# First gate and up weights on a second DMA queue, later loads held, and all roots on GpSimd

## The chip, the cores and the metric

The kernel runs on one core of one Trainium2 chip. The metric is the device time of the whole program in microseconds (us), median of several executions. A profiled execution gives a span that is about 1.7 us shorter than its time, because it runs from the first to the last recorded instruction; times inside the kernel are counted from the start of that span.

TensorE multiplies matrices, VectorE and ScalarE do elementwise work, GpSimd some of the small work. Each takes its instructions in the order in which the program emitted them; below, a normalisation that is ready stands behind statistics that wait 1.49 us for their load. Loads are issued by SyncE, and after the change also by ScalarE; each issuer has a queue of its own (q1 and q10).

## The reference

```python
x = A_x                                   # (1, 2048, 512), bf16
xn = _layernorm(x, axis=-1)               # (x - mean) / sqrt(var + 1e-5)
return x + _A_ref(xn, A_w_r, A_w_i) + _B_ref(xn, B_w_gate, B_w_up, B_w_down)

# _A_ref: irfft2(rfft2(xn) * (w_r + 1j * w_i)), a spectral filter
# _B_ref: g = xn @ w_gate (512 x 1792); u = xn @ w_up (512 x 1792)
#         (gelu_tanh(g) * u) @ w_down (1792 x 512)
```

The rows of x come as 16 tiles of 128 rows, called x0 to x15 here. What matters is the head of the kernel: before TensorE can start on the gate and up products, x0 must be loaded, normalised, transposed on TensorE and copied out of PSUM, and the first 512 columns of `w_gate` (Wg) and `w_up` (Wu) must have landed. One such piece of weights is 512 KB, one tile of x is 128 KB.

## The kernel before

The program does not emit its work directly. It adds operations, with a modelled duration, a key and modelled landing times of the loads (`LAND`, `WG_LAND`, `WU_LAND`), to a list scheduler, which fixes one order per engine.

All first loads are on one queue, in this order:

```python
pin(nc.scalar.activation(out=root[:], in_=eps_t[:], func=AF.Sqrt, ...))  # loads the Sqrt table
load_x(0, 1)
load_x(1, 1)
nc.sync.dma_start(out=idx_t[:], in_=...)      # a table of row numbers, 12 bytes per row
load_w(Wg_sb, 0, 512)
load_w(Wu_sb, 0, 512)
load_x(2, 2)
load_w(Wg_sb, 512, 1024)
load_w(Wu_sb, 512, 1024)
load_x(4, 2)
# [...] more loads
LAND = {0: 2.9, 1: 3.5, 2: 8.8, 3: 8.8}
```

TensorE "spins" on zeros while it waits (N is the number of columns of a product's result). The aim is that its clock is released, that is, let up to full speed, before the real products come. In the traces the starts of products of N=128 are 0.107 us apart at half speed and 0.056 at full speed.

```python
for k in range(25):                           # 20 products of N=128, then 5 of N=512
    pin(nc.tensor.matmul(sp_ps[:, :P if k < 20 else D], lhsT=spin[:],
                         rhs=spin[:] if k < 20 else x_t[:, 0, :], start=True, stop=True))
```

The order on VectorE for the first two tiles (`after=o.get("last")` chains them):

```python
stats(0); mean(0)                             # mean also adds the Sqrt on ScalarE
stats(1)                                      # stands ahead of the first normalisation
recip(0); xn_(0, 0); mean(1); xn_(0, 1)       # xn in two halves of 256 columns
T(0, 0); T(0, 1)                              # transposes on TensorE
add("PE", 0.65, spin_on, ...)                 # six more spin products
copy(0, 0); copy(0, 1)                        # both on VectorE
# [...] the same for tile 1
```

Tiles 2 and 3 follow, with a root by Newton steps on VectorE; then come units of work. A unit is the gate product into a PSUM buffer of tag "G", the gelu of it on ScalarE, the up product into a buffer of tag "U", and on VectorE the product of the two, which frees "U":

```python
g = split("g_ps", "G", Wg_sb, ...)            # acquires one of 2 "G" buffers
u = split("u_ps", "U", Wu_sb, ...)            # acquires one of 2 "U" buffers
ge = add("ACT", ..., f_ge, [g], ..., acq=("ge",), rel=("G",))
h = add("DVE", ..., f_h, [ge, u], ..., rel=("U", "ge"), after=hold.get(k))
```

There are two "U" buffers, so the third up product waits until the first `h` has been done.

## Time and profile before

| | before |
|---|---|
| time, median of 3 (lowest to highest) | 179.57 us (179.57 to 179.84) |
| span of the profiled execution | 177.5 us |
| TensorE busy | 172.1 us, 97 % |
| first gate product starts | 6.34 us |
| first up product starts | 7.79 us |

Engine table of the kernel before: busy us, share of the span, number of instructions.

```profile
PE 172.1 (97%) x1115; PEld 96.0 (54%) x1133; DVE 116.6 (66%) x261; ACT 96.5 (54%) x171; POOL 20.1 (11%) x60
```

TensorE (PE) is the bound. It can only be helped where it idles or works on zeros, that is before about 7.8 us, and at one wait in the middle.

Timeline of VectorE (DVE) before: start us, duration us, engine, line, operation, output<-input, shapes, count, and in brackets the idle time before it with what ended it.

```profile
3.00 0.69 DVE L338 BATCH_NORM_STATS2 stats<-x_t 128x6 f32<-128x512 bf16 x1 [1.99 <-DMA x_t<-in_A_x_dram]
3.82 0.66 DVE L338 BATCH_NORM_STATS2 stats<-x_t 128x6 f32<-128x512 bf16 x1
...
4.58 0.35 DVE L344 TENSOR_SCALAR xn<-x_t,mv,rstd 128x256 bf16<-128x256 bf16 x1
...
8.44 1.29 DVE L338 BATCH_NORM_STATS2 stats<-x_t 128x6 f32<-128x512 bf16 x2 [1.69 <-DMA x_t<-in_A_x_dram]
...
11.46 0.69 DVE L515 TENSOR_TENSOR hT<-u_ps,ge 128x512 bf16<-128x512 f32 x1
```

x0's statistics start at 3.00, x1's at 3.82 with no wait, the first normalisation at 4.58. x2 and x3 land near 8.44, and the first `hT` product (the `h` above) comes at 11.46.

Timeline of TensorE before, same columns.

```profile
5.29 0.56 PE L350 MATMUL tp<-ident_t,xn 128*128 128x128 bf16 x4
...
6.34 0.61 PE L505 MATMUL g_ps<-xnT,Wg_sb 128*128 128x128 bf16 x8
...
7.79 1.07 PE L505 MATMUL u_ps<-xnT,Wu_sb 128*128 128x128 bf16 x16
8.69 1.06 PE L505 MATMUL g_ps<-xnT,Wg_sb 128*128 128x128 bf16 x16
9.59 1.06 PE L505 MATMUL u_ps<-xnT,Wu_sb 128*128 128x128 bf16 x16
10.48 1.91 PE L505 MATMUL g_ps<-xnT,Wg_sb 128*128 128x256 bf16 x16
12.23 0.60 PE L505 MATMUL u_ps<-xnT,Wu_sb 128*128 128x256 bf16 x4
```

Sixteen products of N=128 take 1.07 us, their starts 0.056 us apart: full speed. The 16 gate products of N=256 are two units of 8.

The waits of TensorE before (us in total, times, longest), and two pieces of its chain of waits (start us, us, what).

```profile
PE bp L581 <- ACT Bs L551: 0.4, 1, 0.4
```

```profile
2.65 5.09 DMA Wu_sb<-in_B_w_up_dram
...
7.79 1.07 PE u_ps L505 x16
```

The chain starts with the first up weights, issued at 2.65 and landed 5.09 us later. The wait of 0.4 us (0.45 in the timeline, at 40.4 us) is for a spectral evacuation on ScalarE.

### The profile page before, as it was taken

How to read it: one execution, taken by the hardware profiler on the slowest of the kernel's cores; microseconds unless marked ns; L12 is line 12 of the kernel's file. 1: busy time of each engine (PE TensorE's matmuls, PEld its weight loads, DVE VectorE, ACT ScalarE, POOL GpSimd, SP SyncE). 2: the span in 40 equal slices, each digit the busy share in tenths (PEclk: the TensorE clock that was granted, in tenths of full speed). 3: DMA queues.
4: the chain of work that ended last, by engine and by line, in shares of the span. 5: the costliest groups of instructions: out<-in, count | busy, mean ns of one | idle time of the engine just before them, and what ended most of it. 6: DMA issues, size and time to landing. Idle time of an engine off the chain costs nothing.

```text
span 177.5 us, 3118 instructions
## 1 busy us (share of the span) xinstructions
PE 172.1 (97%) x1115; PEld 96.0 (54%) x1133; DVE 116.6 (66%) x261; ACT 96.5 (54%) x171; POOL 20.1 (11%) x60
## 2 busy tenths in 40 slices
PE   7999999998999999999999999999999999999993
PEld 5798845464455554555555545454445444444463
DVE  3499999873933599998699999543526334344333
ACT  4463286979575989799999955453112111211200
POOL 1000534810676000000000000000000000000000
DMA  3999994243282752121202520200132222221212
GB/s 92 350 382 378 368 180 92 59 98 55 60 291 95 245 173 59 33 55 31 63 6 55 148 60 5 59 0 4 51 97 89 72 78 63 89 85 62 78 44 59
DMA packets 21872, 19.36 MB, mean 109 GB/s; under 512 B 8480, under 2 KB 20000, under 8 KB 21856
## 3 DMA queue, kind: packets, MB, share of 16 engines
q1 hardware_dynamic: 21440, 17.84, 34.6%
q0 software_dynamic: 416, 1.32, 2.5%
q8 instruction: 9, 0.15, 0.3%
q14 instruction: 7, 0.06, 0.1%
HBM read 13.38 MB, written 2.10 MB: 87 GB/s over the span
## 4 chain that ended last, share of the span: by engine, by line
PE 83%; ACT 5%; DMA 3%; issue 3%; POOL 2%; DVE 1%; SPq 1%; ACTq 0%
PE y_ps L820 27%; PE u_ps L505 23%; PE g_ps L505 22%; DMA Wu_sb<-in_B_w_up_dram 3%; PE dp L639 2%; ACT Bs L551 2%; PE yp L772 2%; PE gp L742 2%; PE y_ps L824 2%; PE ep L648 2%; ACT xn L467 2%; ACT ge L510 1%; DVE hT L515 1%; PE bp L581 1%; POOL t L366 0%
## 5 line engine op out<-in xcount | busy, mean ns | idle before, releaser
L505 PE MATMUL u_ps<-xnT,Wu_sb 128*128 128x512 bf16 (+2 forms) x267 | 56.9, 341 | 0.3
L505 PE MATMUL g_ps<-xnT,Wg_sb 128*128 128x512 bf16 (+2 forms) x265 | 56.4, 340 | 0.4
L515 DVE TENSOR_TENSOR hT<-u_ps,ge 128x512 bf16<-128x512 f32 x56 | 38.5, 688 | 19.0 <-PE u_ps L505 10.5
L820 PE MATMUL y_ps<-Wd_sb,hT 128*128 128x512 bf16 (+2 forms) x246 | 50.6, 355 | 0.3
L510 ACT ACTIVATE ge<-g_ps 128x512 bf16<-128x512 f32 x56 | 33.9, 606 | 21.4 <-PE g_ps L505 17.6
L505 PEld LDWEIGHTS <-Wu_sb 128*128 128x128 bf16 x272 | 24.9, 98 | 21.4 <-DMA Wu_sb<-in_B_w_up_dram 0.3
L505 PEld LDWEIGHTS <-Wg_sb 128*128 128x128 bf16 x272 | 24.8, 98 | 20.0
L820 PEld LDWEIGHTS <-hT 128*128 128x128 bf16 x252 | 23.2, 98 | 22.4
L778 ACT CAST yf<-yp 128x512 bf16<-128x512 f32 x16 | 9.3, 586 | 40.5 <-PE yp L772 40.5
L827 DVE TENSOR_TENSOR y_sb<-y_ps,y_sb 128x512 bf16<-128x512 f32 (+2 forms) x18 | 11.1, 631 | 30.0 <-PE y_ps L824 30.0
L653 ACT CAST E<-ep 64x512 bf16<-64x512 f32 x32 | 18.6, 580 | 1.3 <-PE ep L648 0.8
L338 DVE BATCH_NORM_STATS2 stats<-x_t 128x6 f32<-128x512 bf16 x16 | 10.5, 677 | 3.9 <-DMA x_t<-in_A_x_dram 3.9
L467 ACT ACTIVATE xn<-x_t,nb,rstd 128x512 bf16<-128x512 bf16 x12 | 9.7, 827 | 1.8 <-POOL nb L378 1.8
L551 ACT CAST Gs<-gp 128x512 bf16<-128x512 f32 x16 | 8.9, 592 | 0.9 <-PE gp L742 0.9
L551 ACT CAST ds<-dp 128x512 bf16<-128x512 f32 x16 | 9.0, 597 | 0.6 <-PE dp L639 0.5
L551 ACT CAST Bs<-bp 128x512 bf16<-128x512 f32 x16 | 8.4, 607 | 0.5 <-PE bp L581 0.5
L784 DVE TENSOR_TENSOR lv<-yf 128x512 bf16<-128x512 bf16 x16 | 6.1, 422 | 1.5 <-ACT yf L778 0.6
L772 PEld LDWEIGHTS <-Gs 128*128 128x128 bf16 x64 | 4.8, 98 | 3.5
L791 DVE TENSOR_TENSOR yt<-lv 128x512 bf16<-128x512 bf16 x16 | 6.1, 422 | 0.3
L824 PE MATMUL y_ps<-yt,RI_t 128*128 128x512 bf16 (+2 forms) x18 | 6.1, 355 | 0.0
L772 PE MATMUL yp<-CT,Gs 128*128 128x128 bf16 x64 | 6.0, 219 | 0.0
L742 PEld LDWEIGHTS <-F 128*128 128x128 bf16 x64 | 4.5, 98 | 2.6
(72 smaller groups left out, 123.2 us busy)
## 6 DMA issues: line engine op xcount, KB each, us to landing
F<-F SPq DMA_DIRECT2D x32, 64.0 KB, 2.0
y_sb<-in_A_x_dram SPq DMA_DIRECT2D x16, 128.0 KB, 2.1
out_dram<-y_sb SPq DMA_DIRECT2D x15, 128.0 KB, 1.7
x_t<-in_A_x_dram SPq DMA_DIRECT2D x7, 256.0 KB, 8.6
Wd_sb<-in_B_w_down_dram SPq DMA_DIRECT2D x1, 1792.0 KB, 7.5
Wg_sb<-in_B_w_gate_dram SPq DMA_DIRECT2D x2, 512.0 KB, 5.2
Wu_sb<-in_B_w_up_dram SPq DMA_DIRECT2D x2, 512.0 KB, 7.4
Wg_sb<-in_B_w_gate_dram SPq DMA_DIRECT2D x1, 768.0 KB, 10.4
```

Source lines behind the costliest of these rows:

```text
L338: V.bn_stats(out=st[:], in_=x_t[:, c, :])
L467: xn_op[c] = add("ACT", 0.72, lambda c=c: A.activation(out=xn[:, c, :], in_=x_t[:, c, :], func=AF.Identity, bias=nb[:, c:c + 1], scale=rst ...
L505: T_.matmul(b[name][:, f], lhsT=W_[:, e, (f0 + f) * P:(f0 + f + 1) * P], rhs=rhs[:, e, :], start=(e == 0), stop=(e == NE - 1))
L510: A.activation(out=b["ge"][:], in_=b["g_ps"][:], func=AF.Gelu_apprx_tanh)
L515: V.tensor_tensor(out=hT_of(sb, f0, m, o, w), in0=b["u_ps"][:], in1=b["ge"][:], op=ALU.mult)
L551: A.copy(out=o, in_=i)
L653: A.copy(out=b["E"][64 * h:64 * h + 64, r], in_=b["ep", h][64 * r:64 * r + 64])
L772: T_.matmul(t[:, q], lhsT=late["G"][:, q, c0 + j], rhs=IQ[q], start=(q == 0), stop=(q == 3), skip_group_check=True)
L778: A.copy(out=b["yf"][:, j], in_=b[j][:])
L820: T_.matmul(b[o][:], lhsT=hT_of(sb, f, 1, cl * P, P)[:, 0], rhs=Wd_sb[:, f, o:o + w], start=(f == 0), stop=False)
L824: T_.matmul(b[o][:], lhsT=late["RI"][:, c, :], rhs=late["yt"][:, c, o:o + w], start=False, stop=True)
L827: V.tensor_tensor(out=b["y"][:, o:o + w], in0=b[o][:], in1=b["y"][:, o:o + w], op=ALU.add)
```

## The change

Its intent: use the time before 7.8 us better. The first weights are to start at 0.8 us on ScalarE's queue instead of at 2.18 and 2.65 us; the later loads are held until the first root, so that they do not compete. The roots go to GpSimd's `pow`, so that ScalarE needs no Sqrt table and loads the gelu table early. The first unit is halved along its contraction, so that it can start on half of x0's transposed data.

```diff
-    pin(nc.scalar.activation(out=root[:], in_=eps_t[:], func=AF.Sqrt, bias=eps_t[:], scale=1.0))
+    nc.gpsimd.memset(Wg_sb[0:1, 0, 0:1], 0.0)            # before the identity is built
+    load_w(Wg_sb, 0, 512, nc.scalar)
+    load_w(Wu_sb, 0, 512, nc.scalar)
+    pin(nc.scalar.activation(out=warm[:], in_=eps_t[:], func=AF.Gelu_apprx_tanh))
     load_x(0, 1)
     load_x(1, 1)
-    nc.sync.dma_start(out=idx_t[:], ...)
-    load_w(Wg_sb, 0, 512)
-    load_w(Wu_sb, 0, 512)
-    load_x(2, 2)
-    load_w(Wg_sb, 512, 1024)
-    load_w(Wu_sb, 512, 1024)
+    def later_loads():
+        load_w(Wg_sb, 512, 1024)
+        load_x(2, 2)                                      # now behind the second gate weights
+        load_w(Wu_sb, 512, 1024)
+        # [...] the rest as before, idx_t late
-    LAND = {0: 2.9, 1: 3.5, 2: 8.8, 3: 8.8}
+    LAND = {0: 2.9, 1: 3.8, 2: 8.2, 3: 8.2}
-    for k in range(25):                                   # 20 x N=128, 5 x N=512
+    for k in range(32):                                   # 32 x N=128
# [...]
-            nc.tensor.matmul(sp_ps[:, :256], ...)         # spin_on
+            nc.tensor.matmul(sp_ps[:, :P], ...)
# [...] first_two():
         stats(0)
         mean(0)
         stats(1)
-        recip(0)
+        def rest():
+            nc.gpsimd.memset(Wg_sb[0:1, 0, 512:513], 0.0)
+        g = add("POOL", 0.15, rest, [o["root", 0]], key=-1999)
+        add("SP", 9.0, later_loads, [g], key=-1000)       # the hold
         xn_(0, 0)
-        mean(1)
         xn_(0, 1)
+        mean(1)
# [...]
+    def root(c0, n):                                      # for all tiles
+        nc.gpsimd.tensor_tensor(out=y, in0=y, in1=minus_half[:, 0:n], op=ALU.pow)
# [...] unit(): first unit halved, and the order of h on VectorE is free
+        if k == 0:
+            g = add("PE", occ / 2, lambda: mm_half(0), [xT_op[0, 0]], ...)
+            g = add("PE", occ / 2, lambda: mm_half(1), [xT_op[0], g], ...)
-        h = add("DVE", ..., rel=("U", "ge"), after=hold.get(k))
+        h = add("DVE", ..., rel=("U", "ge"))
```

Left out are the copies of the transposed halves (now one on VectorE, one on ScalarE) and the first output, split into four pieces.

The memset of one element of `Wg_sb` makes the load that overwrites it wait for GpSimd; this is how the later loads are held (the memset runs at 4.83 us, and the second gate weights are issued at 4.95).

More of the change, by code (lines that the diff above doesn't have):

```diff
@@ L261 @@
     spin = pc.tile([P, P], BF16, name="spin")
-    root = pc.tile([P, 1], F32, name="root")
+    warm = pc.tile([P, 1], F32, name="warm")
     nc.vector.memset(spin[:], 0.0)
     nc.vector.memset(eps_t[:], EPS)
+    minus_half = pc.tile([P, 4], F32, name="minus_half")
+    nc.vector.memset(minus_half[:], -0.5)
     ident_t = pc.tile([P, P], BF16, name="ident_t")
     nc.gpsimd.memset(ident_t[:], 1.0)
+    nc.gpsimd.memset(Wg_sb[0:1, 0, 0:1], 0.0)
     nc.gpsimd.affine_select(out=ident_t[:], in_=ident_t[:], pattern=[[-1, P]], compare_op=ALU.is_equal, fill=0.0,
@@ L281 @@
     idx_t = pc.tile([P, 3], I32, name="idx_t")
-    nc.sync.dma_start(out=idx_t[:], in_=nc.inline_tensor(idx_np, name="spec_rows").ap())
-    load_w(Wg_sb, 0, 512)
-    load_w(Wu_sb, 0, 512)
-    load_x(2, 2)
-    load_w(Wg_sb, 512, 1024)
-    load_w(Wu_sb, 512, 1024)
-    load_x(4, 2)
-    load_x(6, 2)
-    load_w(Wg_sb, 1024, DF)
-    load_w(Wu_sb, 1024, DF)
-    load_x(8, 2)
-    load_x(10, 2)
-    for c in range(0, NC, 8):
-        nc.sync.dma_start(out=RF_t[:, c:c + 8], in_=rf_d.rearrange("p (c k) -> p c k", c=NC)[:, c:c + 8])
@@ L296 @@
-    load_x(12, 2)
-    load_x(14, 2)
-    load_consts("F0", "L0")
-    load_consts("I0", "M0")
-    LAND = {0: 2.9, 1: 3.5, 2: 8.8, 3: 8.8}
-    LAND.update({c: 12.6 if c < 8 else 18.5 if c < 12 else 21.5 for c in range(4, NC)})
-    WG_LAND = [6.6] * 4 + [10.2] * 4 + [15.0] * 6
-    WU_LAND = [8.0] * 4 + [11.7] * 4 + [17.0] * 6
-    RF_LAND = 20.0
-    for T, w_in in ((TR, A_w_r), (TI, A_w_i)):
-        rows = w_in.rearrange("(kb a h g) k -> h kb a (g k)", kb=NC, h=2, a=8)
-        Tf = T.rearrange("p j k -> p (j k)")
-        for h in range(2):
-            nc.sync.dma_start(out=Tf[64 * h:64 * h + 64, W:8 * W], in_=rows[h, :, 0:4, W:8 * W])
+    def later_loads():
+        load_w(Wg_sb, 512, 1024)
+        load_x(2, 2)
+        load_w(Wu_sb, 512, 1024)
+        load_x(4, 2)
+        load_x(6, 2)
+        load_w(Wg_sb, 1024, DF)
+        load_w(Wu_sb, 1024, DF)
+        load_x(8, 2)
+        load_x(10, 2)
+        for c in range(0, NC, 8):
+            nc.sync.dma_start(out=RF_t[:, c:c + 8], in_=rf_d.rearrange("p (c k) -> p c k", c=NC)[:, c:c + 8])
+        load_x(12, 2)
+        load_x(14, 2)
+        nc.sync.dma_start(out=idx_t[:], in_=nc.inline_tensor(idx_np, name="spec_rows").ap())
+        load_consts("F0", "L0")
+        load_consts("I0", "M0")
+        for T, w_in in ((TR, A_w_r), (TI, A_w_i)):
+            rows = w_in.rearrange("(kb a h g) k -> h kb a (g k)", kb=NC, h=2, a=8)
+            Tf = T.rearrange("p j k -> p (j k)")
+            for h in range(2):
+                nc.sync.dma_start(out=Tf[64 * h:64 * h + 64, W:8 * W], in_=rows[h, :, 0:4, W:8 * W])
@@ L312 @@
+    LAND = {0: 2.9, 1: 3.8, 2: 8.2, 3: 8.2}
+    LAND.update({c: 11.5 if c < 8 else 17.5 if c < 12 else 20.5 for c in range(4, NC)})
+    WG_LAND = [5.4] * 4 + [7.5] * 4 + [13.2] * 6
+    WU_LAND = [6.4] * 4 + [9.6] * 4 + [15.2] * 6
+    RF_LAND = 19.0
     ident = ident_t[:]
@@ L316 @@
     sp_ps = ps.tile([P, D], F32, name="sp_ps", tag="S", bufs=4)
-    for k in range(25):
-        pin(nc.tensor.matmul(sp_ps[:, :P if k < 20 else D], lhsT=spin[:], rhs=spin[:] if k < 20 else x_t[:, 0, :],
-                             start=True, stop=True))
+    for k in range(32):
+        pin(nc.tensor.matmul(sp_ps[:, :P], lhsT=spin[:], rhs=spin[:] if k < 20 else x_t[:, 0, :P], start=True,
+                             stop=True))
     def spin_on():
         for k in range(6):
-            nc.tensor.matmul(sp_ps[:, :256], lhsT=spin[:], rhs=x_t[:, 0, :256], start=True, stop=True)
+            nc.tensor.matmul(sp_ps[:, :P], lhsT=spin[:], rhs=x_t[:, 0, :P], start=True, stop=True)
     plan = Plan({"S": 4, "G": 2, "U": 2, "ge": 3, "A": 1, "xf": 2, "ds": 4, "E": 2, "X": 2, "Y": 2, "F": 2,
@@ L353, in f_Tc, with plus_eps, root_eps, bias @@
         copy(out=xnT[0][:, e0:e0 + n, c, :], in_=tiles["T", c, e0][:])
-    def rsqrt_steps(U, c0, n):
+    def plus_eps(U, c0, n):
+        U.tensor_scalar(out=rstd[:, c0:c0 + n], in0=mv[:, c0:c0 + n, 1], scalar1=EPS, scalar2=None, op0=ALU.add)
+    def root(c0, n):
         y = rstd[:, c0:c0 + n]
-        v = pc.tile([P, n], F32, name=f"v{c0}")
-        t = pc.tile([P, n], F32, name=f"t{c0}")
-        def first():
-            U.tensor_scalar(out=v[:], in0=mv[:, c0:c0 + n, 1], scalar1=EPS, scalar2=None, op0=ALU.add)
-            U.tensor_scalar(out=y.bitcast(I32), in0=v[:].bitcast(I32), scalar1=-0.5, scalar2=float(0x5F1FFFF9),
-                            op0=ALU.mult, op1=ALU.add)
-        def newton(a, k):
-            U.tensor_tensor(out=t[:], in0=y, in1=y, op=ALU.mult)
-            if U is V:
-                U.scalar_tensor_tensor(out=t[:], in0=v[:], scalar=-a, in1=t[:], op0=ALU.mult, op1=ALU.mult)
-                U.scalar_tensor_tensor(out=y, in0=t[:], scalar=k, in1=y, op0=ALU.add, op1=ALU.mult)
-                return
-            U.tensor_tensor(out=t[:], in0=v[:], in1=t[:], op=ALU.mult)
-            U.tensor_scalar(out=t[:], in0=t[:], scalar1=-a, scalar2=k, op0=ALU.mult, op1=ALU.add)
-            U.tensor_tensor(out=y, in0=t[:], in1=y, op=ALU.mult)
-        def bias():
-            b = nb[:, c0:c0 + n]
-            U.tensor_tensor(out=b, in0=mv[:, c0:c0 + n, 0], in1=y, op=ALU.mult)
-            U.tensor_scalar(out=b, in0=b, scalar1=-1.0, scalar2=None, op0=ALU.mult)
-        steps = [first, lambda: newton(0.703952253, 0.703952253 * 2.38924456), lambda: newton(0.5, 1.5)]
-        return steps + ([] if U is V else [bias])
+        nc.gpsimd.tensor_tensor(out=y, in0=y, in1=minus_half[:, 0:n], op=ALU.pow)
+    def root_eps(c0, n):
+        plus_eps(nc.gpsimd, c0, n)
+        root(c0, n)
+    def bias(c0, n):
+        U, b = nc.gpsimd, nb[:, c0:c0 + n]
+        U.tensor_tensor(out=b, in0=mv[:, c0:c0 + n, 0], in1=rstd[:, c0:c0 + n], op=ALU.mult)
+        U.tensor_scalar(out=b, in0=b, scalar1=-1.0, scalar2=None, op0=ALU.mult)
     xn_op, xT_op = {}, {}
@@ L391, in v @@
             o["last"] = o[k]
-        def root_of(c):
-            o["root", c] = add("ACT", 0.31, lambda: A.activation(
-                out=rstd[:, c:c + 1], in_=mv[:, c, 1:2], func=AF.Sqrt, bias=eps_t[:], scale=1.0),
-                [o["mean", c]], key=-2000 + c)
         def T(c, h):
@@ L400, in T @@
                                lat=0.36, acq=("S",))
-        def recip(c):
-            v(("rstd", c), lambda: V.reciprocal(out=rstd[:, c:c + 1], in_=rstd[:, c:c + 1]), 0.15, [("root", c)])
         def xn_(c, h):
-            v(("xn", c, h), lambda: f_norm_v(c, 256 * h, 256), 0.27, [("rstd", c)], lat=0.4)
-        def copy(c, h):
-            v(("copy", c, h), lambda: f_Tc(c, 2 * h, 2), 0.25, [("T", c, h)], lat=0.4)
-            o["copy", c, h].rel = ("S",)
+            v(("xn", c, h), lambda: f_norm_v(c, 256 * h, 256), 0.27, [("root", c)], lat=0.4)
         def stats(c):
@@ L415, in mean @@
         def mean(c):
-            v(("mean", c), lambda: f_mean(c), 0.1, [("stats", c)])
-            root_of(c)
+            v(("mean", c), lambda: f_mean(c), 0.17, [("stats", c)])
+            v(("eps", c), lambda: plus_eps(V, c, 1), 0.09, [("mean", c)], lat=0.25)
+            o["root", c] = add("POOL", ROOT, lambda: root(c, 1), [o["eps", c]], key=-2000 + c, lat=ROOT + 0.1)
         stats(0)
@@ L421, in first_two @@
         stats(1)
-        recip(0)
+        def rest():
+            nc.gpsimd.memset(Wg_sb[0:1, 0, 512:513], 0.0)
+        g = add("POOL", 0.15, rest, [o["root", 0]], key=-1999)
+        add("SP", 9.0, later_loads, [g], key=-1000)
         xn_(0, 0)
+        xn_(0, 1)
         mean(1)
-        xn_(0, 1)
-        table = add("ACT", 1.3, lambda: None, [o["root", 1]], key=-1500, lat=1.3)
         T(0, 0)
         T(0, 1)
-        add("PE", 0.65, spin_on, [o["T", 0, 1]], key=-1500, lat=0.65, after=o["T", 0, 1])
-        copy(0, 0)
-        copy(0, 1)
-        recip(1)
-        v("xn1", lambda: f_norm_v(1, 0, D), 0.33, [("rstd", 1)], lat=0.45)
+        add("PE", 0.33, spin_on, [o["T", 0, 1]], key=-1500, lat=0.33, after=o["T", 0, 1])
+        v("copy0", lambda: f_Tc(0, 0, 2), 0.25, [("T", 0, 0)], lat=0.4)
+        o["copy0"].rel = ("S",)
+        xT_op[0, 0] = o["copy0"]
+        xT_op[0] = add("ACT", 0.36, lambda: f_Tc(0, 2, 2, A.copy), [o["T", 0, 1]], key=-1300, lat=0.48, rel=("S",))
+        xn_op[0] = o["xn", 0, 1]
+        v("xn1", lambda: f_norm_v(1, 0, D), 0.33, [("root", 1)], lat=0.45)
         t = add("PE", 0.23, lambda: f_T(1, 0, NE), [o["xn1"]], key=-1998, lat=0.45, acq=("S",))
-        xT_op[0], xn_op[0] = o["copy", 0, 1], o["xn", 0, 1]
-        xT_op[1] = add("ACT", 0.5, lambda: f_Tc(1, 0, NE, A.copy), [t, table], key=-1200, rel=("S",))
+        o["t"] = t
+        v("copyt", lambda: f_Tc(1, 0, NE), 0.5, ["t"])
+        o["copyt"].rel = ("S",)
+        xT_op[1] = o["copyt"]
         xn_op[1] = o["xn1"]
+    ROOT = 0.5
     first_two()
@@ L443, in moments @@
         return add("DVE", 0.1, lambda: f_mean(c), [s], key=key - 0.5)
-    hold = {}
     def second_two():
         m = [moments(c, -1200 + c) for c in (2, 3)]
-        steps = rsqrt_steps(V, 2, 2)
-        m = [add("DVE", 1.5, lambda: [f() for f in steps], m, key=-1190)]
-        hold[0] = m[0]
+        m = add("POOL", ROOT, lambda: root_eps(2, 2), m, key=-1190, lat=ROOT + 0.1)
         for c in (2, 3):
-            xn_op[c] = add("DVE", 0.33, lambda c=c: f_norm_v(c, 0, D), m, key=-1180 + c, lat=0.53)
-            hold[1] = xn_op[c]
+            xn_op[c] = add("DVE", 0.33, lambda c=c: f_norm_v(c, 0, D), [m], key=-1180 + c, lat=0.53)
             t = add("PE", 0.23, lambda c=c: f_T(c, 0, NE), [xn_op[c]], key=-880 + c, lat=0.5, acq=("S",))
@@ L462, in later_four @@
         m = [moments(c, km + 0.1 * c) for c in range(c0, c0 + 4)]
-        for k, f in enumerate(rsqrt_steps(nc.gpsimd, c0, 4)):
-            m = [add("POOL", (0.8, 1.15, 1.15, 0.7)[k], f, m, key=c0 + k,
-                     lat=(0.8, 1.15, 1.15, 0.9)[k])]
+        m = [add("POOL", ROOT, lambda: root_eps(c0, 4), m, key=c0, lat=ROOT + 0.1)]
+        m = [add("POOL", 0.7, lambda: bias(c0, 4), m, key=c0 + 1, lat=0.9)]
         for c in range(c0, c0 + 4):
@@ L470, in later_four @@
             xT_op[c] = add("SP", 1.3, lambda c=c: nc.sync.dma_start_transpose(
-                out=xnT[c // 4][:, :, c % 4, :], in_=xn[:, c, :]), [xn_op[c]], key=c, lat=4.0, t_min=25.0)
+                out=xnT[c // 4][:, :, c % 4, :], in_=xn[:, c, :]), [xn_op[c]], key=c, lat=4.0, t_min=24.0)
     later_four(4, 10, 5)
@@ L506, in mm, with mm_half @@
                               start=(e == 0), stop=(e == NE - 1))
+        def mm_half(s):
+            if s == 0:
+                b["g_ps"] = ps.tile([P, m, w], F32, name="g_ps", tag="G", bufs=2)
+            for e in (2 * s, 2 * s + 1):
+                for f in range(m):
+                    T_.matmul(b["g_ps"][:, f], lhsT=Wg_sb[:, e, (f0 + f) * P:(f0 + f + 1) * P], rhs=rhs[:, e, :],
+                              start=(e + f == 0), stop=(e == NE - 1), skip_group_check=True)
         def f_ge():
@@ L524, in split @@
             return o
-        g = split("g_ps", "G", Wg_sb, 1000 + k, WG_LAND, 2 if k == 0 else m)
-        u = split("u_ps", "U", Wu_sb, 1000.5 + k, WU_LAND, 1 if k == 2 else m)
+        if k == 0:
+            g = add("PE", occ / 2, lambda: mm_half(0), [xT_op[0, 0]], key=1000, acq=("G",), t_min=WG_LAND[0])
+            g = add("PE", occ / 2, lambda: mm_half(1), [xT_op[0], g], key=1000.1, lat=occ / 2 + 0.3)
+        else:
+            g = split("g_ps", "G", Wg_sb, 1000 + k, WG_LAND, m)
+        u = split("u_ps", "U", Wu_sb, 1000.5 + k, WU_LAND, (2, m, 1)[k] if k < 3 else m)
         ge = add("ACT", {1: 0.28, 2: 0.36, 4: 0.5}[n * m], f_ge, [g], key=-1000 + k,
                  lat={1: 0.38, 2: 0.48, 4: 0.7}[n * m], acq=("ge",), rel=("G",))
-        h = add("DVE", {1: 0.21, 2: 0.34, 4: 0.61}[n * m], f_h, [ge, u], key=-1000 + k, rel=("U", "ge"),
-                after=hold.get(k))
+        h = add("DVE", {1: 0.21, 2: 0.34, 4: 0.61}[n * m], f_h, [ge, u], key=-1000 + k, rel=("U", "ge"))
         for c in range(c0, c0 + n):
@@ L815, in load, with mm @@
             nc.sync.dma_start(out=b["y"][:], in_=x_v[:, c, :])
-        def mm(o, w):
-            b[o] = ps.tile([P, w], F32, name="y_ps", tag="S", bufs=4)
-            for f in range(NFC):
+        def mm(o, w, fs):
+            if 0 in fs:
+                b[o] = ps.tile([P, w], F32, name="y_ps", tag="S", bufs=4)
+            for f in fs:
                 T_.matmul(b[o][:], lhsT=hT_of(sb, f, 1, cl * P, P)[:, 0], rhs=Wd_sb[:, f, o:o + w],
@@ L834, in down @@
             k = 2000 + 10 * c + o / D
-            m = add("PE", 14 * w * 0.000421, lambda o=o, w=w: mm(o, w), [h_op[c, f] for f in range(NFC)] + [wd],
-                    key=k, acq=("S",))
+            m, n = [h_op[c, f] for f in range(NFC)] + [wd], 1 if c else 4
+            for i in range(n):
+                fs = range(i * NFC // n, (i + 1) * NFC // n)
+                m = [add("PE", len(fs) * w * 0.000421, lambda o=o, w=w, fs=fs: mm(o, w, fs), m, key=k,
+                         acq=() if i else ("S",))]
+                m[0].lat = m[0].occ
+            m = m[0]
             r = add("PE", w * 0.000421, lambda o=o, w=w: ri_mm(o, w), [m, yt_op[c], ri], key=k + 0.1,
                     lat=w * 0.000421 + 0.3)
-            m.lat = m.occ
             t = add("DVE", 0.1 + w * 0.001, lambda o=o, w=w: total(o, w), [r, x], key=k, rel=("S",))
```

## The prediction

> **What bounds the kernel now.** TensorE: 172.1 of 177.5 us busy (engine table). In the timeline it spins from 1.05 us, starts the first gate product at 6.34 us, and from the first up product at 7.79 us to the last near 174.7 us it is nearly gapless: by windows about 1.4 us idle, of which one real wait, 0.45 us at 40.4 us, for a spectral evacuation on ScalarE (the rest are 0.05 us holes, probably missing records). The chain of waits begins with the first up weights (issued 2.65 us, landing 5.09 us later), then is TensorE. So the change can win only what lies before 7.79 us, plus that 0.45 us.
>
> **What the change does, costed.**
> 1. First gate and up weights move to ScalarE's queue at about 0.8 us instead of 2.18 and 2.65 us. In fine windows the DMA moves only 19 to 86 GB/s from 3.0 to 4.0 us and then 240 to 385; that hole is filled. x0, x1 and both weights are 1.28 MB, at about 350 GB/s from 2.0 us done near 5.8 us (estimate), so the 0.31 us wait for the up weights goes. The built order shows the up load first on that queue, beside x0. As the Trainium skill says (DMA: Bandwidth & Descriptors, "Issuing engines are not separate DMA queues"), all queues share the same engines, so x0 (now at 3.0 us) and x1 should come 0 to 0.4 us later.
> 2. The root leaves ScalarE (0.29 us) and the VectorE reciprocal (0.15): now a VectorE add (about 0.17) and a GpSimd pow. Small GpSimd operations take 0.20 us here; pow I guess 0.25 to 0.5, plus hand-overs of 0.05 to 0.1. The first normalisation moves from 4.58 to 4.7 to 5.0 us, also because the second statistics (0.66 us) stand ahead of it on VectorE.
> 3. The two transposed halves are copied on VectorE and ScalarE in parallel, not serially (0.49 us for both), and the gate product starts on the first half: about 0.25 us back. First gate product 6.1 to 6.5 us.
> 4. The gelu table (1.28 us at 7.85) is loaded early; the first gelu moves from 9.14 to about 7.4 us. Off TensorE's path.
> 5. Then 16 gate products (0.9 us), a transpose (0.23), and up at 7.2 to 7.6 us instead of 7.79: 0.2 to 0.55 us won.
> 6. Later loads held until the first root (about 5 us) land as early or 0.5 us earlier; gate columns 512 to 1023 are needed only near 10 us.
> 7. The new order puts two gate/up pairs between the middle spectral groups (was one and a half), 3.4 us against 2.8 us of ScalarE work: the 0.45 us wait probably goes. The first output split into four is neutral.
>
> Sum: 0.3 to 1.0 us, middle 0.7.
>
> **Predicted: 178.9 us, 8 in 10 between 178.0 and 179.7. Faster by over 2%: 0.02; within 2%: 0.96; slower: 0.02.**
>
> **Right if** the up product starts at 7.2 to 7.6 us with no DMA wait, x0's statistics at 3.0 to 3.4 us, pow takes under 0.5 us, and the wait near 40 us is gone.
>
> **Wrong if** (a) pow costs over 1 us: the start is late by as much; (b) the weights delay x0 more; (c) the clock is not released: the Trainium skill (TensorE: Matmul & The Clock Gate, Part 1) wants a busy window of about 3.4 us. This trace agrees: weight loads take 151 ns until 4.44 us, 102 from 4.98. The new warm-up is about 3.4 us of cold products (32 x 0.107, estimate), then a gap; half speed to 8 us would cost about 1 us; (d) reordering opens new evacuation waits between 25 and 110 us.

## The result, and the profile after

| | before | after |
|---|---|---|
| time, median (lowest to highest) of 4 runs each | 179.57 us (179.44 to 179.84) | 180.83 us (180.56 to 180.88) |
| ratio after/before, 95 % interval | | 1.0065 (1.0048 to 1.0083) |
| span of the profiled execution | 177.5 us | 178.8 us |
| x1's statistics start | 3.82 | 5.68 |
| first normalisation starts | 4.58 | 6.29 |
| first gate product starts | 6.34 | 7.77 |
| first up product starts | 7.79 | 9.73 |
| x2's statistics start | 8.44 | 10.93 |

Ratios here are the mean time of one kernel's fast runs over the mean of the other's fast runs of the same rounds, so they differ a little from the ratio of the medians quoted.

It is within 2 %, as predicted, but it is slower, and outside the predicted 178.0 to 179.7. Engine table after:

```profile
PE 172.0 (96%) x1122; PEld 97.4 (54%) x1140; DVE 115.6 (65%) x254; ACT 94.4 (53%) x168; POOL 18.4 (10%) x42
```

No engine has noticeably more work. So the time is lost in waits and in the speed of TensorE. Timeline of VectorE after:

```profile
3.10 0.69 DVE L343 BATCH_NORM_STATS2 stats<-x_t 128x6 f32<-128x512 bf16 x1 [2.08 <-DMA x_t<-in_A_x_dram]
...
5.68 0.70 DVE L343 BATCH_NORM_STATS2 stats<-x_t 128x6 f32<-128x512 bf16 x1 [1.49 <-DMA x_t<-in_A_x_dram]
6.29 0.59 DVE L349 TENSOR_SCALAR xn<-x_t,mv,rstd 128x256 bf16<-128x256 bf16 x2
...
10.93 1.29 DVE L343 BATCH_NORM_STATS2 stats<-x_t 128x6 f32<-128x512 bf16 x2 [0.57 <-DMA x_t<-in_A_x_dram]
12.13 0.30 DVE L346 BATCH_NORM_AGGREGATE mv<-stats 128x2 f32<-128x6 f32 x2
12.35 1.28 DVE L508 TENSOR_TENSOR hT<-u_ps,ge 128x512 bf16<-128x512 f32 x2
```

x0 is only 0.10 us later. But x1 is not there until 5.66, and VectorE waits 1.49 us for it. The normalisation of x0 does not need x1; it only stands behind x1's statistics. The root was ready before (GpSimd's `pow` for x0 runs from 4.28 for 0.58 us).

Timeline and wait of TensorE after:

```profile
3.16 1.49 PE L323 MATMUL sp_ps<-x_t,spin 128*128 128x128 bf16 x12
6.68 0.65 PE L355 MATMUL tp<-ident_t,xn 128*128 128x128 bf16 x4 [2.04 <-DVE xn L349]
...
7.77 1.91 PE L498 MATMUL g_ps<-xnT,Wg_sb 128*128 128x128 bf16 x16
9.47 0.42 PE L355 MATMUL tp<-ident_t,xn 128*128 128x128 bf16 x4
9.73 1.06 PE L490 MATMUL u_ps<-xnT,Wu_sb 128*128 128x128 bf16 x16
...
12.41 1.04 PE L490 MATMUL g_ps<-xnT,Wg_sb 128*128 128x256 bf16 x8
13.29 0.93 PE L490 MATMUL u_ps<-xnT,Wu_sb 128*128 128x256 bf16 x7
```

```profile
PE tp L355 <- DVE xn L349: 2.0, 1, 2.0
```

TensorE idles 2.04 us and then runs its first 16 gate products at half speed: 1.91 us for what takes 1.06 us a moment later. Their starts are 0.107 us apart until about 9.6 us and 0.056 after it. The Trainium skill (TensorE: Matmul & The Clock Gate, Part 1) gives these very spacings for the held and the released clock and asks for a busy window of about 3.4 us. The spacings agree with the trace; the window no run here shows as such (in all of them the products start at 1.05 us, and the release comes anywhere from 4.1 us in e10 to past 11 in e1). The wait of 0.4 us near 40 us is gone, as predicted: it is not in the list of waits any more.

The chain of waits after, its head:

```profile
1.25 4.41 DMA x_t<-in_A_x_dram
...
5.68 0.70 DVE stats L343
```

x1 was issued at 1.25, as before (1.24), and took 4.41 us. Why? The DMA view, cut to two stretches, gives for each queue the packets, the MB and the share of 16 engines; q1 is SyncE's queue, q10 is ScalarE's. First from 2.75 to 4.0 us, then from 4.2 to 5.0 us, both of the kernel after:

```profile
q10 hardware_dynamic: 320, 0.33, 88.3%
```

```profile
q10 hardware_dynamic: 177, 0.16, 59.0%
q1 hardware_dynamic: 139, 0.13, 49.2%
```

From 2.75 to 4.0 us not one packet of SyncE's queue was served, although x1 had been issued there at 1.25. What was served is Wu, issued by ScalarE at 0.80. x1's 0.13 MB came only when Wu was nearly through. The prediction had let x1 share the engines with the weights, at a cost of 0 to 0.4 us; the trace shows it standing behind nearly all of Wu (ScalarE's queue had moved 0.46 of Wu's 0.52 MB by 4.2 us, when x1's packets began in earnest).

The account: the first up product starts 1.94 us later (9.73 against 7.79). The span is 178.8 - 177.5 = 1.3 us longer. So about 0.6 us come back after that point, of which the wait at 40 us is 0.45.

### The profile page after: what moved, and what is told of

Its sections match the earlier page's. It is cut to its first block, busy times and chain, and to the rows that moved or that the text cites. A ratio compares the mean times of both kernels' runs of the same rounds, so it can differ in the third digit from the quotient of the medians.

```text
span 178.8 us, 3105 instructions
## 1 busy us (share of the span) xinstructions
PE 172.0 (96%) x1122; PEld 97.4 (54%) x1140; DVE 115.6 (65%) x254; ACT 94.4 (53%) x168; POOL 18.4 (10%) x42
## 3 DMA queue, kind: packets, MB, share of 16 engines
q10 hardware_dynamic: 1056, 1.05, 1.8%
## 4 chain that ended last, share of the span: by engine, by line
PE 94%; DMA 2%; DVE 1%; issue 1%; SPq 0%
PE y_ps L817 27%; PE u_ps L490 27%; PE g_ps L490 27%; DMA x_t<-in_A_x_dram 2%; PE dp L635 2%; PE yp L768 2%; PE bp L577 2%; PE gp L738 2%; PE y_ps L821 2%; PE ep L644 2%; PE g_ps L498 1%; PE tp L355 1%; DVE stats L343 0%; PE sp_ps L328 0%; SPq L274 0%
## 5 line engine op out<-in xcount | busy, mean ns | idle before, releaser
L490 PEld LDWEIGHTS <-Wg_sb 128*128 128x128 bf16 x256 | 24.0, 98 | 20.8
L452 ACT ACTIVATE xn<-x_t,nb,rstd 128x512 bf16<-128x512 bf16 x12 | 9.2, 804 | 1.4 <-POOL nb L374 1.4
L681 DVE TENSOR_TENSOR m<-X,TW 128x1024 bf16<-128x1024 bf16 x8 | 5.5, 688 | 0.2
```

The costliest lines, as they stand in the source:

```text
L452: xn_op[c] = add("ACT", 0.72, lambda c=c: A.activation(out=xn[:, c, :], in_=x_t[:, c, :], func=AF.Identity, bias=nb[:, c:c + 1], scale=rst ...
L490: T_.matmul(b[name][:, f], lhsT=W_[:, e, (f0 + f) * P:(f0 + f + 1) * P], rhs=rhs[:, e, :], start=(e == 0), stop=(e == NE - 1))
```

## The experiments

Several things happened together in the head; the theory at first had two parts:

- **A**: x1 lands late behind Wu, its statistics stand ahead of x0's normalisation, and everything starts late.
- **B**: the warm-up is shorter (32 short products instead of 20 short and 5 long) and followed by 2 us of idling, so the clock is held until 9.6 us.

The rivals: GpSimd's `pow` is what costs; or ScalarE's queue is served by preference, whatever the order. "Before" in a ratio is always the kernel before on the same chip in the same rounds.

### e1_x1_first: x1 onto ScalarE's queue ahead of the weights

```diff
-    load_w(Wg_sb, 0, 512, nc.scalar)
-    load_w(Wu_sb, 0, 512, nc.scalar)
+    pin(load_x(1, 1, nc.scalar))
+    pin(load_w(Wu_sb, 0, 512, nc.scalar))
+    pin(load_w(Wg_sb, 0, 512, nc.scalar))
...
-    load_x(1, 1)
```

> Changed kernel, with the second x tile issued on ScalarE's queue ahead of the up and gate weights. Theory (the second x tile is served after the 512 KB of up weights because loads are served in the order of issue, whatever their queue): x1 lands at 3.4 to 3.9 us instead of 5.66, its statistics no longer hold up VectorE, the first normalisation starts near 4.95 us (was 6.29), the first gate product is then held only by the gate weights (about 7.1 us), up starts at 8.0 to 8.4 us (was 9.73); time 178.9 to 179.8 us. Rival 1 (the loss is the unreleased TensorE clock alone): about 180.1 us or more, gate products still 0.107 us apart. Rival 2 (GpSimd pow, 0.58 us, is what makes the start late): no change, 180.8 us.

Measured: 180.67 us (180.17 to 181.34), ratio 1.0058 (1.0032 to 1.0084). The time missed what A expected, and by itself it fits what was written for rival 1, the clock alone. The wait for x1 is gone (its statistics follow at 5.18 without a wait), but now x0 came late: its statistics start at 4.17, because the last packets of x0 trickled in on SyncE's queue until about 3.8 us while x1 and Wu flowed on the other. The first normalisation starts at 5.97, and in the profiled run, the slowest of the runs, products were 0.107 us apart until past 11 us. So this run moved the lateness from x1 to x0 instead of taking it away. It also shows that the loads are not simply served one queue after the other.

### e2_stats_behind: x1's statistics behind the normalisation of x0

```diff
-  v(("xn", c, h), lambda: f_norm_v(c, 256 * h, 256), ...)
+  v(("xn", c, h), lambda: (f_norm_v(c, 256 * h, 256), h and f_stats(1)), ...)
-  v(("stats", c), lambda: f_stats(c), ...)
+  v(("stats", c), lambda: c or f_stats(c), ...)
```

> Changed kernel, with the second statistics moved behind the first tile's two normalisations in VectorE's order; nothing else moves. Theory: x1 still lands near 5.66 us, but the first normalisation starts at 4.9 to 5.0 us; the gate product starts when the gate weights land, about 7.1 us, so 0.6 to 1.3 us are won: 179.5 to 180.2 us. Rival 1 (clock alone): under 0.3 us won. If the late x1 itself and not its place on VectorE were the matter, the second tile's chain would hold the second unit instead and nothing is won: 180.8 us.

Measured: 180.20 us (180.10 to 180.60), ratio 1.0046 (1.0021 to 1.0070). Only an order on VectorE was changed. The first normalisation moves from 6.29 to 4.96 us:

```profile
4.96 0.60 DVE L349 TENSOR_SCALAR xn<-x_t,mv,rstd 128x256 bf16<-128x256 bf16 x2 [0.70 <-POOL rstd L365]
```

The gate product then waits 0.33 us for Wg and starts at 6.99, still at half speed until about 9.8 us, and the first up product starts at 9.09 instead of 9.73. So the order on VectorE is worth 0.6 us at that point. The time is at the upper end of what was expected; by the ratio it is 0.3 us better than the change (1.0046 against 1.0065), with intervals that overlap. The normalisation at 4.96 us also shows that the `pow` is not the trouble: with it the path from x0's statistics to the normalisation is 1.80 us (3.16 to 4.96), against 1.58 (3.00 to 4.58) before. It costs 0.22 us. (e11, where x1's statistics stand ahead as they do before, has the same 1.80: 2.97 to 4.77.)

### e3_long_spin: seven more long products of zeros, nothing else

```diff
+    for k in range(7):
+        pin(nc.tensor.matmul(sp_ps[:], lhsT=spin[:], rhs=x_t[:, 0, :], start=True, stop=True))
```

> Changed kernel, with seven more 512-wide warm-up products, so that TensorE is busy until about 6.6 us instead of 4.6. x1 still lands near 5.66 us and the first normalisation is at 6.29 us. Theory: the clock is released before the first gate product, the 16 gate products are 0.056 us apart instead of 0.107, up starts near 8.9 us instead of 9.73: 180.0 us (179.8 to 180.3). If the clock is no cost: 180.8 us. If the clock is all of the loss: 179.0 us.

Measured: 179.85 us (179.61 to 180.19), ratio 1.0017 (0.9993 to 1.0041). TensorE of this run:

```profile
7.53 1.05 PE L500 MATMUL g_ps<-xnT,Wg_sb 128*128 128x128 bf16 x16
...
8.65 1.06 PE L492 MATMUL u_ps<-xnT,Wu_sb 128*128 128x128 bf16 x16
```

The same 16 gate products now take 1.05 us instead of 1.91. From first gate to first up product it is 1.12 us instead of 1.96. The ratio falls by 0.0048, about 0.9 us. B is real, and by the medians the larger of the two mends, although x1 was as late as ever (statistics at 5.80). A first sign of something else: a new wait of 0.3 us of the third up product for `hT`.

### e4_queue_alone: the kernel before, with only the weights moved to ScalarE's queue

```diff
+    pin(load_w(Wu_sb, 0, 512, nc.scalar))
+    pin(load_w(Wg_sb, 0, 512, nc.scalar))
     pin(nc.scalar.activation(out=root[:], in_=eps_t[:], func=AF.Sqrt, ...))
...
-    load_w(Wg_sb, 0, 512)
-    load_w(Wu_sb, 0, 512)
```

> Kernel before, with one part of the change alone: first up and gate weights issued on ScalarE's queue ahead of its table load; root, copies, warm-up and later loads as before. Theory: x1 again lands near 5.6 us, its statistics again stand ahead of the first normalisation on VectorE (now near 6.3 us, was 4.58), up starts at 8.6 to 9.5 us instead of 7.79: 180.4 to 181.3 us, so this part alone explains the loss. Rival (the hold, pow or the shorter warm-up are to blame): 179.0 to 179.6 us.

Measured: 181.31 us (180.41 to 182.09), ratio 1.0118 (1.0071 to 1.0164). x0's statistics start at 3.84, x1's at 5.63, the first normalisation at 6.43. There is no `pow` in this kernel, and the late start is there. So the moved weights alone make the late start.

```profile
5.63 0.69 DVE L338 BATCH_NORM_STATS2 stats<-x_t 128x6 f32<-128x512 bf16 x1 [0.88 <-DMA x_t<-in_A_x_dram]
...
6.43 0.34 DVE L344 TENSOR_SCALAR xn<-x_t,mv,rstd 128x256 bf16<-128x256 bf16 x1
```

In this execution they make it without the slow clock: the warm-up is that of the kernel before, eight gate products take 0.61 us as they did there, and still the first up product starts at 9.04 instead of 7.79 and the span is 1.2 us longer (178.7 against 177.5). The four runs fall into two groups (180.41 and 180.60; 182.02 and 182.09), and the profile is of the first.

### e5_weights_behind_x: the weights stay on ScalarE's queue, but are issued after x1

The memsets of one element of Wg and of Wu stand behind the building of the identity, so that the two loads are issued at 1.45 and 1.90 us, Wg first now.

```diff
-    nc.gpsimd.memset(Wg_sb[0:1, 0, 0:1], 0.0)
     nc.gpsimd.affine_select(out=ident_t[:], ...)
+    tc.keep_in_program_order(nc.gpsimd.memset(Wg_sb[0:1, 0, 0:1], 0.0))
+    tc.keep_in_program_order(nc.gpsimd.memset(Wu_sb[0:1, 0, 0:1], 0.0))
```

> Changed kernel, with the first gate and up weights still on ScalarE's queue, but held until GpSimd has made the identity (about 1.5 us), so that both x tiles are issued before them. Warm-up as changed. Theory: x0 lands at 3.0 to 3.3 us and x1 at 3.6 to 4.2 us (5.66 in the changed kernel), the first normalisation starts near 4.95 us, the first gate product at 6.1 to 6.5 us. If the shorter warm-up leaves the clock unreleased until after 8 us, up starts near 8.1 us and the time is 179.1 to 179.6 us; if the clock is released by then, up starts near 7.3 us and the time is 178.5 to 178.9 us. Rival (ScalarE's queue is preferred to SyncE's whatever the order): x1 stays behind the weights, above 5 us, and the time near 180.5 us.

Measured: 180.65 us (179.95 to 182.30), ratio 1.0067 (1.0026 to 1.0107). The early start is back: x1's statistics at 4.22, first normalisation at 4.87, gate at 6.45 at full speed, up at 7.86. ScalarE's queue is not preferred: x1, issued ahead of the weights, was served ahead of them. (e1 shows that the order of issue is not the whole rule: x0 was issued early there and came late.)

```profile
3.16 1.37 PE L324 MATMUL sp_ps<-x_t,spin 128*128 128x128 bf16 x12
...
6.45 1.05 PE L499 MATMUL g_ps<-xnT,Wg_sb 128*128 128x128 bf16 x16 [0.30 <-POOL rstd L366]
```

Nor was the warm-up mended here: it is that of the change. The clock was released at its very end (its last 12 products take 1.37 us; in the change they take 1.49, all at half speed), and stayed released over the idle time that followed. e2, with the same warm-up and the same 0.7 us of idle time after it, stayed at half speed. So the short warm-up does not always miss the release, and its length alone does not settle part B. One execution of each was profiled; why they differ is not shown. And yet the time is no better than that of the change. The reason stands in the list of waits of TensorE:

```profile
PE u_ps L491 <- DVE hT L509: 1.6, 1, 1.6
```

What A and B had cost was back, and it was lost again at the third up product. So A and B are not the whole theory.

### e6_behind_and_spin and e7_sync_queue_and_spin

e6 is e5 with two more long spin products. e7 has the weights on SyncE's queue right behind x0 and x1, and the same two products; the hold of the later loads is kept in both.

```diff
# e6, on top of e5
+    for k in range(2):
+        pin(nc.tensor.matmul(sp_ps[:], lhsT=spin[:], rhs=x_t[:, 0, :], start=True, stop=True))
# e7, on top of the change
-    load_w(Wg_sb, 0, 512, nc.scalar)
-    load_w(Wu_sb, 0, 512, nc.scalar)
-    load_x(0, 1)
-    load_x(1, 1)
+    pin(load_x(0, 1))
+    pin(load_x(1, 1))
+    pin(load_w(Wg_sb, 0, 512))
+    pin(load_w(Wu_sb, 0, 512))
+    # the same two long spin products
```

> As the run with the weights held behind x, with two more 512-wide warm-up products that keep TensorE busy until about 5.3 us, as in the kernel before. Theory: both losses are gone; gate products 0.056 us apart, up starts at 7.2 to 7.6 us, time 178.4 to 178.9 us, below both kernels. If something else in the change costs time (pow, the hold of the later loads), it stays at 179.4 us or more.

> The changed kernel with the queue part undone: first gate and up weights on SyncE's queue right behind x0 and x1 (the row table stays late), with the same two more warm-up products. Theory: the order of issue is what matters, not the queue: x1 at 3.6 to 4.0 us, up at 7.2 to 7.7 us, time within 0.3 us of the run with the weights held behind x on ScalarE's queue. If the second queue itself gains something, this one is slower by more than 0.3 us.

Measured: e6 180.24 us (179.72 to 180.96), ratio 1.0042 (1.0015 to 1.0070); e7 180.35 us (180.07 to 182.32), ratio 1.0070 (1.0032 to 1.0108). Gate and up start at 6.52 and 7.64 in e6, at 6.31 and 7.42 in e7. e6 missed its forecast of 178.4 to 178.9 us and fell into the other branch, 179.4 or more, "if something else in the change costs time". The two agree within their intervals, so the queue itself matters little. Both lose time in the same wait, 1.29 us in e6 and 1.45 in e7. VectorE and TensorE in e7:

```profile
10.44 1.29 DVE L345 BATCH_NORM_STATS2 stats<-x_t 128x6 f32<-128x512 bf16 x2 [2.39 <-DMA x_t<-in_A_x_dram]
11.64 0.30 DVE L348 BATCH_NORM_AGGREGATE mv<-stats 128x2 f32<-128x6 f32 x2
11.86 1.27 DVE L510 TENSOR_TENSOR hT<-u_ps,ge 128x512 bf16<-128x512 f32 x2
```

```profile
10.11 1.04 PE L492 MATMUL g_ps<-xnT,Wg_sb 128*128 128x256 bf16 x8
12.59 1.03 PE L492 MATMUL u_ps<-xnT,Wu_sb 128*128 128x256 bf16 x8 [1.45 <-DVE hT L510]
```

This is how it comes about. The third up product needs a "U" buffer, which the first `hT` frees. On VectorE `hT` stands behind the statistics of x2 and x3. These wait 2.39 us for their load, which the change holds until the first root, and puts behind the second gate weights. The kernel before had the same order on VectorE, but x2-3 at 8.44 us and one more gate unit on TensorE to fill the time.

This gives part **C**: late x2-3 set a second limit on the third up product, at about 12.6 us, which in the change (13.29) is hidden behind A and B, and shows as soon as they are mended.

### e8_before_rows_late: a control on the kernel before

The kernel before with only its row table `idx_t` loaded late, as the change does it. (The diff is that one line, moved behind the loads of x.)

> Kernel before with one edit: the small row table is loaded late, so the first gate and up weights are issued 0.47 us earlier on SyncE's queue. Theory: the hole in the DMA traffic at 3.0 to 4.0 us shrinks, the 0.31 us wait for the up weights goes, up starts at 7.4 to 7.6 us instead of 7.79: 0.2 to 0.4 us faster than before, the wait of 0.4 us near 40 us stays. If earlier weights delay x: slower than before.

Measured: 179.16 us (178.97 to 179.62), ratio 0.9988 (0.9966 to 1.0010). The first up product starts at 7.63 with no wait for its load, the wait near 40 us stays. By its median it is 0.16 us faster, less than the 0.2 to 0.4 forecast, and the interval contains 1: this part of the change is not shown to be worth anything.

### e9_x2_first: the change, with x2-3 ahead of the second gate weights

```diff
     def later_loads():
-        load_w(Wg_sb, 512, 1024)
         load_x(2, 2)
+        load_w(Wg_sb, 512, 1024)
         load_w(Wu_sb, 512, 1024)
# [...] held as before, by one more memset
+            nc.gpsimd.memset(x_t[0:1, 2, 0:1], 0.0)
```

> The changed kernel with one thing altered: the loads of tiles x2 and x3 go ahead of the second gate weights (still held until root 0). Theory: two late paths run side by side in the changed kernel. The first is the late first normalisation (x1 behind the up weights in the loads, its statistics ahead of the normalisation on VectorE) with a half-speed TensorE until 9.5 us; the second is x2-3 landing near 10.9 us, with their statistics ahead of the product that frees the first up buffer. With the first left as it is, mending the second alone gives little: statistics of x2 at 8.7-9.2 us instead of 10.93, first normalisation still 6.2-6.4, first up product still 9.5-9.8, time 180.4-180.9. Rival: the late x2-3 are the whole loss; then the time falls to 179.2-179.7.

Measured: 180.96 us (180.59 to 181.16), ratio 1.0093 (1.0079 to 1.0108). First normalisation at 6.10, up at 9.63. The statistics of x2 start at 10.17, later than expected, but without a wait for the load: ahead of them stands a copy that waits for TensorE until 9.83. Mending C alone gives nothing, as the theory has it; the time is even 0.06 us above the expected range. The rival, that late x2-3 are the whole loss, is refuted.

### e10_e6_x2_first: e6 with x2-3 ahead of the second gate weights

The edit is that of e9, made on e6.

> The kernel e6 (weights behind the x tiles, two more long spin products) with x2-3 ahead of the second gate weights, still held until root 0. Theory: e6 had the early start back (first gate 6.5, up 7.6) and lost it again in the 1.3 us wait of the third up product for the buffer that the VectorE frees behind the statistics of x2-3. Expect x2's statistics at 7.8-8.7 us, that wait under 0.3 us, and 178.7-179.4 (against 180.24 for e6). Rival: the wait comes from something else in the chain of the first units; then it stays over 1 us and the time over 180.

Measured: 179.44 us (178.83 to 180.25), ratio 1.0006 (0.9984 to 1.0027), against 1.0042 for e6. x2's statistics start at 8.48. The waits of TensorE from 2 us on:

```profile
PE g_ps L494 <- DMA Wg_sb<-in_B_w_gate_dram: 0.5, 1, 0.5
PE tp L358 <- DVE xn L352: 0.4, 1, 0.4
PE u_ps L494 <- DMA Wu_sb<-in_B_w_up_dram: 0.3, 1, 0.3
```

The wait for `hT` is gone. In its place there are 0.5 and 0.3 us for the second weights, which the hold makes start late. (Of these the 0.3 stays in e11, which has no hold.) The time is that of the kernel before, 0.04 us above what was expected.

### e11_no_hold: e7 with no hold and x2-3 first

```diff
# on top of e7
     def later_loads():
-        load_w(Wg_sb, 512, 1024)
         load_x(2, 2)
+        load_w(Wg_sb, 512, 1024)
         load_w(Wu_sb, 512, 1024)
# [...]
-        def rest():
-            nc.gpsimd.memset(Wg_sb[0:1, 0, 512:513], 0.0)
-        g = add("POOL", 0.15, rest, [o["root", 0]], key=-1999)
-        add("SP", 9.0, later_loads, [g], key=-1000)
+        add("SP", 9.0, later_loads, [], key=-1000)
```

> The kernel e7 (weights on the sync queue behind x0 and x1, two more long spin products) with no hold on the later loads and x2-3 first among them: the load order of the kernel before without its row table, with everything else of the change (power roots, halved first unit, split copies, split last unit) kept. Theory: the loads' order and hold are the whole loss, the rest of the change is worth its 0.4-0.6 us: first up 7.3-7.6, x2's statistics 7.9-8.5, the wait of the third up product under 0.3, 178.5-179.2, that is 0.2-0.8 below the kernel before. Rival: the power roots on GpSimd and the split copies cost as well; then the time is that of the kernel before or above it, 179.4-180.

Measured: 178.94 us (178.80 to 179.00), ratio 0.9976 (0.9963 to 0.9988). Every number fell in its range: first up product at 7.35, x2's statistics at 8.17, no wait for `hT`. The waits of TensorE from 2 us on are one line:

```profile
PE u_ps L488 <- DMA Wu_sb<-in_B_w_up_dram: 0.5, 2, 0.3
```

So with the loads in the order of before (without its row table), the first weights on SyncE's queue, two more spin products, and everything else of the change kept, the kernel is faster than before by 0.24 %. The power roots, the halved first unit and the split copies do not cost anything that shows. The sum: 0.44 us from the earlier up product (7.79 to 7.35) and 0.45 from the wait at 40 us, less 0.34 for the second of the two waits above, makes 0.55; the spans differ by 0.6 (177.5 and 176.9). Of the 0.44, the late row table may account for 0.16: e8, with that alone, has the up product at 7.63.

### e12_no_hold_old_order: e7 with only the hold taken away

The edit is the second half of e11's; x2-3 stay behind the second gate weights.

> The kernel e7 with only the hold taken away: the later loads are issued straight behind the first weights, and x2-3 still stand behind the second gate weights as in the change. With e7 (hold, that order: 180.35), e10 (hold, x2-3 first: 179.44) and e11 (no hold, x2-3 first: 178.94) this fills the table of two by two. Estimate from the traces: x2's statistics began at 8.17 us in e11; 512 KB more ahead of them at the 290 GB/s of e11's first 14 us are 1.8 us, so 9.7-10.1 us; the first product on VectorE 1.42 us later (as in e7, 10.44 to 11.86), at 11.1-11.5, ends 0.7 later, so that the third up product starts at 11.8-12.2 in place of e11's 11.42, with a wait of 0.7-1.2 us for VectorE. Theory (what counts is when x2-3 land, by either cause): 179.2-179.8. Rival (the hold alone is the second loss, the order is free): 178.8-179.1.

Measured: 179.56 us (179.34 to 179.85), ratio 1.0011 (0.9997 to 1.0026). One of the eleven runs of the kernel before in these rounds took 230.15 us; it is not counted. VectorE's statistics of x2 and TensorE's third up product in this run:

```profile
9.45 1.29 DVE L345 BATCH_NORM_STATS2 stats<-x_t 128x6 f32<-128x512 bf16 x2 [1.78 <-DMA x_t<-in_A_x_dram]
```

```profile
11.60 1.03 PE L488 MATMUL u_ps<-xnT,Wu_sb 128*128 128x256 bf16 x8 [0.62 <-DVE hT L506]
```

The time is in the theory's range (179.2 to 179.8) and not in the rival's (178.8 to 179.1). The instants are 0.2 to 0.3 us earlier than the early end of the estimate. With it the two causes of late x2-3 can be set side by side, all with the early start and the two more spin products, as ratios to the kernel before:

| | x2-3 behind the second gate weights | x2-3 first |
|---|---|---|
| later loads held | e7 1.0070 (e6: 1.0042) | e10 1.0006 |
| not held | e12 1.0011 | e11 0.9976 |

The hold and the order each cost about 0.3 to 0.6 %. (e10 has the weights on ScalarE's queue, the others in the table on SyncE's; its direct neighbour is e6. The ratios come from three sets of rounds, on three chips.)

## Why the prediction was right or wrong

**Right: TensorE is the bound, and only the head and the wait near 40 us can be won** (first paragraph, item 7). The wait is gone in the profile after and stays away in e11.

**Wrong, and the step that failed first: item 1**, "x0 (now at 3.0 us) and x1 should come 0 to 0.4 us later". x0 came 0.10 us later, x1 1.86 us (5.68 against 3.82). The prediction took from the Trainium skill (DMA: Bandwidth & Descriptors, "Issuing engines are not separate DMA queues") that the loads share the same engines. The trace agrees in so far as the two queues moved 0.16 and 0.13 MB side by side from 4.2 to 5.0 us. But the prediction then took it that a small load gets its share at once. The trace shows x1 behind nearly all 512 KB of Wu: at the 0.33 MB per 1.25 us measured there, 512 KB take 2 us. e4, with this one part of the change in the kernel before, shows the whole late start (first normalisation at 6.43 instead of 4.58). That x0 itself was hardly late is not sure to hold in another execution: in e3 and e4, with the same weights issued at 0.80 us, its statistics started at 3.96 and 3.84.

**Item 2 was right in the cost, wrong in what it rested on.** It noted that "the second statistics (0.66 us) stand ahead of it on VectorE" and charged 0.66 us for them. That is their work; their wait is also ahead of it. The normalisation came at 6.29 instead of 4.7 to 5.0. e2, which moves only this, has it at 4.96, inside the range. The `pow` was guessed at 0.25 to 0.5 us and took 0.58, so the condition "pow takes under 0.5 us" failed by a little, with no weight in the result.

**Items 3 to 5 fell with them**: the gate product started at 7.77 instead of 6.1 to 6.5, the first gelu at 9.71 instead of 7.4, the up product at 9.73 instead of 7.2 to 7.6. In e11 the gate product starts at 5.90 and the up product at 7.35.

**Warning (c) was right, and should have been counted.** The prediction wrote that half speed to 8 us "would cost about 1 us"; half speed lasted to about 9.6, and e3 puts its cost at about 0.9 us. It was listed as a way to be wrong and given no weight in the range, although it is more than the middle (0.7 us) of the predicted gain. The reading behind it was also off. It took shorter weight loads from 4.98 us for the clock's release. One load at 4.98 us is short, but those at 5.29 to 5.50 take 151 ns again, and the products of the kernel before are still 0.107 us apart at 5.3 to 5.6 us. The spacing of the products is the mark to use. That the early release in e11 is due to its two more spin products was not tested by itself, and e5 was released without them.

**Item 6 was the second failed step**: "Later loads ... land as early or 0.5 us earlier". x2-3 came 2.5 us later (statistics at 10.93 against 8.44). The hold was counted as free, but it has their load issued at 5.38 us instead of 3.20, and the second gate weights, 512 KB, now go ahead of it. In the change itself this is hidden (e9), but it takes away all that a mended start would give (e5, e6, e7), and e10 to e12 show both of its causes, the hold and the order. The prediction checked only when the second gate weights are needed, not the "U" buffer that VectorE frees behind x2's statistics.

**The sum.** Predicted -0.3 to -1.0 us. Measured +1.26 us by the medians. The first up product, predicted at 7.2 to 7.6, started at 9.73; about 0.6 us came back later.

What stays open: why a load of 128 KB stands behind 512 KB on another queue while, in e1, x0 and x1 are served side by side from two queues. The trace tells when packets moved, not when they were ready to move, so the issue of descriptors and the choice between queues can't be told apart. Nor do these traces show when the clock's window begins, so the release (about 9.6 us in the change, past 11 in e1, near 5.5 in e3, 4.3 in e5) is seen but not derived.

## What to carry to other kernels

Here a second queue gave no gain (e6 and e7 agree): it only changed who was served first, and a small urgent load ended up behind a big one that was issued 0.45 us earlier. Put the loads in the order of need; on one queue that order comes without a hold, and here it was the fastest (e11). On VectorE, which works in order, the 1.49 us wait for x1 was paid by all that stood behind it; so look at the order of each engine for work that is ready but stands behind work whose load may be late, and after mending one late path, look for the next one behind it.

## What the Trainium skill lacked or had wrong

- DMA: Bandwidth & Descriptors, "Queues, rings and completion order", says that each engine round-robins between the queues it has work for, packet by packet. Here from 2.75 to 4.0 us ScalarE's queue moved 320 packets and SyncE's none, with x1 issued there at 1.25 us. Either x1's descriptors were not yet there, or the turns are not even; the page should say what to expect of a small load issued behind a big one on another queue. In e1 the packets of two queues were mixed (74 and 48 from 2.0 to 2.5 us).
- No page that we used tells that the last few packets of a load can trail by 1 us beside a big load: with the same loads x0's packets had all been served by 2.75 us in the change and its statistics started at 3.10; in e3 seven of its packets came between 3 and 4 us, and its statistics started at 3.96.
- TensorE: Matmul & The Clock Gate, Part 1, tells the clock by the spacing of products, and that agrees (0.107 and 0.056 us). The granted clock in the record does not show it: it reads 1.00 in the stretch below, of the change, from 8 to 10 us (its columns: stretch, us, busy us of the five engines with counts, granted clock, DMA share, GB/s), while its products were 0.107 us apart until about 9.6 us.

```profile
8.00:10.00 2.00, 2.00 (x25) 2.00 (x24) 0.30 (x2) 0.29 (x1) 0.00 (x0) 1.00 1.01 330
```

- GPSIMD Engine Reference has no duration for `pow`: 0.55 to 0.58 us for 128x1.
